# A third tile for raw weights, fixed places for block inputs and g, inputs loaded a block ahead, and stores issued later, in a fused attention and MLP kernel

## The chip, the cores and the metric

The kernel runs on one core of a Trainium2 chip. The metric is the device time in microseconds (us) of one execution; the number compared is the median over runs. TensorE is called PE in the profile, VectorE DVE, ScalarE ACT, GpSimd POOL, and SyncE, from whose queue every load and store of this kernel is issued, SP.

## The reference

Four batches of eight heads go through an attention with 512 local and 32 global tokens (a local token sees the global ones and a window of 32 to either side), then through two MLPs. Here is what the two MLPs compute, with x of 4 x 544 = 2176 tokens by 512:

```
h = np.maximum(x @ w_in, 0.0)          # 512 x 2048
x = h * h @ w_out                      # 2048 x 512
a = x @ w1;  b = x @ w2                # 512 x 1024 each
y = (a * b @ w3) @ w_out2              # 1024 x 1024, 1024 x 512
```

The weights arrive as 64-bit floats.

## The kernel before

**Numbers.** Every product on PE is made of three passes in a fast fp32 mode over a high and a low part of both factors (`PASSES`), so each tensor that PE reads is kept as a pair of parts, written by ACT (the high part, a cast) and DVE (the low part, a subtraction).

**Conversions.** The 72 weight tiles of 128 x 512 come as 64-bit raw tiles (`wraw`, 512 KB each). `conv(n)` turns one into a pair: two ACT instructions read the raw tile (L399 and L402, in `conv_a`), two DVE instructions follow (L407 and L412, `conv_b`; L412 reads the raw tile last), then POOL adds (L477, or L466 for the last 16), ACT casts (L422) and DVE subtracts (L423). `conv_b(n)` also issues the load of raw tile n + 2, since there are two places with the tag `wraw`. One `conv(n)` is `conv_c(n - 1)`, `conv_b(n)`, `conv_a(n + 1)`, so each raw tile is held from its `conv_a` to the `conv_b` of the next call. For n from 16 on, the first ACT and the first DVE instruction of a conversion are held in the order in which the program was written.

**Blocks.** The 2176 tokens are eight blocks of 256 or 288. The first MLP's 2048 hidden columns are done in two halves. The first half runs over blocks 0 to 7, beside the attention up to block 5; its result is stored to `part_d`, and the pair of each input block to `xs_d`. The second half runs over blocks 0 to 7 again with the weights 16 to 31: the pair comes back from `xs_d` (`load_split`, L512), the partial sum from `part_d` (`load_x`, L650), and the sum goes to `x2_d` (L712). The trace names the stored sum `x_d<-st`.

Blocks 6 and 7 of the first half, and all blocks of the second, are written out by `rows`: for f from 0 to 8 a `h_unit` (12 matmuls into one of two PSUM tiles `h`, then on ACT L521 relu, L522 square to the high part of `g`, L528 square again, then on DVE L127 the low part) and an `x_add` for the f before it (12 matmuls into four `acc`). Between f = 4 and f = 7 the four pieces of the next block's input are split or loaded. These inputs and the eight `g` of a block come from 14 places that are given out in turn (tag `hl`). `end_b` then adds `acc` and the partial sum on DVE (L710), stores, and loads the partial sum of the block after next.

**Work beside the blocks.** `merge` spreads the conversions 16 to 29 over the steps of blocks 6 and 7, and 30 to 71 over the second half. With the conversions 41 to 56 go 16 `w_unit` steps (12 matmuls of 512 columns each), which multiply w3 with the last weight in advance; every second one copies its PSUM tile to SBUF on ACT (L702, tile `ws`, which takes a place of the tag `wraw`) and stores it to `w_d` (L703). The conversions 56 to 71 make w1 and w2 in pairs: the first four pairs are stored at once (`both_d`, `sums_d`, L471 and L472).

**After that** come a and b (products by blocks, seven instead of eight, L727), four passes over the units, and y. In the last pass weight pieces are loaded (L905, L919) and split at steps that the table `LATE_V` sets: a row for each quarter of the pass, a number of steps after each of the seven products.

The order on each engine is not that of the code alone: a scheduler places instructions whose operands are ready by its own reckoning.

Of the kernel before, what the change touches and what calls it, by code (L numbers as in the profile page):

```python
# [9 lines left out]
F32 = mybir.dt.float32  # L10
F32R = mybir.dt.float32r
BF16 = mybir.dt.bfloat16
I32 = mybir.dt.int32
# [36 lines left out]
NB = 288  # L50
NBLK = 2 * B
# [3 lines left out]
def block(i):  # L55
    i %= NBLK
    return S * (i // 2) + HALF * (i % 2), HALF if i % 2 == 0 else S - HALF
# [7 lines left out]
RUNS = (0, 16, PAIRED + 16)  # L65
# [14 lines left out]

AHEAD = ((0, 0, 0, 0, 0, 0, 0), (1, 0, 1, 0, 1, 0, 1), (1, 0, 1, 0, 1, 0, 1), (2, 1, 2, 0, 2, 1, 2))
LATE_W = ((2, 1, 1, 0, 2, 1, 1), (1, 1, 1, 1, 1, 1, 1), (1, 1, 1, 0, 1, 0, 0))
LATE_V = ((1, 0, 0, 0, 0, 0, 0), (2, 1, 2, 0, 2, 1, 1), (2, 1, 2, 0, 2, 1, 2), (0, 0, 0, 0, 0, 0, 0))

SHARED = 6

# [6 lines left out]
def attention_mlp(ctx: ExitStack, tc: tile.TileContext, kq0, kq, vw, wts, mask, ident, out_d):  # L93
    nc = tc.nc
# [7 lines left out]
    sb = ctx.enter_context(pool("sb"))  # L102
    cv_cm, rot_cm, at_cm = pool("cv"), pool("rot", "right"), pool("at", "right")
    cv, rot, at = cv_cm.__enter__(), rot_cm.__enter__(), at_cm.__enter__()
# [36 lines left out]
    x_t = {}  # L141
# [241 lines left out]

    raw_t, mid_t, w_t = {}, {}, {}

    def load_w(n):
        t = pools["cv"].tile([128, 512, 2], I32, tag="wraw", name="wraw", bufs=2)
        if n >= PAIRED:
            k, u = divmod(n - PAIRED, 2)
            at = PAIRED + 2 * (LATE + FIRST)[k] + u  # L390
        else:
            at = n
        nc.sync.dma_start(out=t, in_=wts[at].bitcast(I32).rearrange("p (c w) -> p c w", w=2))
        raw_t[n] = t
# [10 lines left out]
    def conv_b(n):  # L405
        raw, (a, b, _) = raw_t.pop(n), mid_t[n]
        first = nc.vector.tensor_scalar(  # L407
            out=a, in0=a, scalar1=3, scalar2=0x7FFFFFF8, op0=ALU.logical_shift_left, op1=ALU.bitwise_and
        )
        if n >= RUNS[1]:  # L410
            tc.keep_in_program_order(first)
        nc.vector.scalar_tensor_tensor(  # L412
            out=b, in0=raw[:, :, 1], scalar=-(1 << 31), in1=a, op0=ALU.bitwise_and, op1=ALU.bitwise_or
        )
        if n + 1 not in RUNS and n + 2 not in RUNS:
            load_w(n + 2)

    def unit(tag, dtype=F32R):
        return pools[tag].tile([128, 2, 512], dtype, tag=tag, name=tag, bufs=16)
# [40 lines left out]
    def conv_c(n):  # L460
        _, b, m = mid_t.pop(n)
        if n >= PAIRED:
            k, u = divmod(n - PAIRED, 2)
            if u == 0:
                both_t[k] = unit("u1", F32)
            nc.gpsimd.tensor_tensor(out=both_t[k][:, u].bitcast(I32), in0=b, in1=m, op=ALU.add)  # L466
            if u == 1:
                x = both_t.pop(k)
                s = add_up(x, "u1", nc.vector)
                if k < 4:  # L470
                    nc.sync.dma_start(out=both_d[k], in_=x)  # L471
                    nc.sync.dma_start(out=sums_d[k], in_=s)  # L472
                else:
                    for f in split_blocks(FIRST[k - 4], k, x, s, "u1"):
                        f()
            return
        nc.gpsimd.tensor_tensor(out=b, in0=b, in1=m, op=ALU.add)  # L477
        t = w_t[n] = unit(UNITS[n])
        split_w(t, slice(0, 512), b.bitcast(F32))
# [16 lines left out]
    def parts(n):  # L496

        return sb.tile([128, 2, NB], F32R, tag="hl", name="hl", bufs=HL_BUFS)[:, :, :n]

    def of_split(i, k):  # L500
        s, n = block(i)
        return xs_d[:, k, :, s : s + n]

    def split_x(i, k, src):
        t = xh[i, k] = parts(src.shape[-1])
        nc.scalar.copy(t[:, 0], src)
        split_lo(nc.vector, t[:, 1], src, t[:, 0])
        nc.sync.dma_start(out=of_split(i, k), in_=t.bitcast(F32))

    def load_split(i, k):  # L510
        t = xh[NBLK + i, k] = parts(block(i)[1])
        nc.sync.dma_start(out=t.bitcast(F32), in_=of_split(i, k))  # L512

    def h_unit(i, f, w):
        n = block(i)[1]
        h = ps.tile([128, 512], F32, tag="h", name="h", bufs=H_BUFS)[:, :n]
        w = w_t[w]
        chain(h, [(w[:, a, 128 * k : 128 * (k + 1)], xh[i, k][:, b]) for k in range(4) for a, b in PASSES])
        r = sb.tile([128, NB], F32, tag="tmp", name="r", bufs=4)[:, :n]
        g = g_t[f] = parts(n)  # L520
        nc.scalar.activation(r, h, AF.Relu)  # L521
        nc.scalar.activation(g[:, 0], r, AF.Square)  # L522
        if i < SHARED:
            nc.vector.scalar_tensor_tensor(
                out=r, in0=h, scalar=0.0, in1=r, op0=ALU.max, op1=ALU.mult
            )
        else:
            nc.scalar.activation(r, r, AF.Square)  # L528
        split_lo(nc.vector, g[:, 1], r, g[:, 0])
# [29 lines left out]
                    start=(f + k == 0), stop=(f + k == 9),  # L559
                )  # L560

    def rows(i, w_in, w_out, split, end):

        n = block(i)[1]
        steps = []
        for f in range(9):
            if f < 8:
                steps.append(lambda f=f: h_unit(i, f, w_in + f))
            if 4 <= f < 8:
                steps.append(lambda f=f: split(f - 4))  # L570
            if f > 0:
                steps.append(lambda f=f: x_add(i, f - 1, w_t[w_out + f - 1], n))
        steps.append(lambda: [end(d) for d in range(4)])
        return steps

    def of(t, i):
        s, n = block(i)
        return t[:, :, s : s + n]
# [67 lines left out]
    def load_x(i):  # L646

        if i < NBLK:
            t = x_t[i] = sb.tile([128, 4, NB], F32, tag="xb", name="xl", bufs=2)[..., : block(i)[1]]
            nc.sync.dma_start(out=t, in_=of(part_d, i))  # L650

    for i in range(0, NBLK, 2):
        main = []
        for j in (i, i + 1):
            if j >= SHARED:
                main += rows(
                    j, 0, 8, lambda d, j=j: split_a(j + 1, d), lambda d, j=j: end_a(j, d, acc[d])
                )
                continue
            if j > 0:  # L660
                main += [lambda f=f, j=j: h_unit(j, f, f) for f in range(8)]
            main += [lambda d=d, j=j: x_unit_a(j, d) for d in range(4)]
        b = i // 2 + 1
        if b < B:
            if b == 1:
                cv_cm.__exit__(None, None, None)
                cv_cm = pool("sp")
                pools["cv"] = cv_cm.__enter__()
                load_kq(H // 2)
                for k in range(H, H + 4):  # L670
                    load_v(k)
            steps = [s for j in range(4 * b - 1, 4 * b + 4) for s in cycle(j, j < 4 * b + 3, j >= 4 * b)]
            fills = [(steps, 0, len(main) - 5)]
        else:
            for cm in (at_cm, rot_cm, cv_cm):
                cm.__exit__(None, None, None)
            pools["u2"] = ctx.enter_context(pool("u2", "right"))
            cv_cm = pool("cv2")
            pools["cv"] = cv_cm.__enter__()
            load_w(16)  # L680
            load_w(17)
            main.insert(18, lambda: load_x(0))
            fills = [([lambda n=n: conv(n) for n in range(16, 30)], 0, len(main))]
        merge(main, *fills)
# [3 lines left out]

    def w_unit(f, half):
        if half == 0:  # L690
            wacc[f] = ps.tile([128, 512], F32, tag="x", name="wacc", bufs=X_BUFS)
        o = wacc[f]
        w3 = w_t[40 + 2 * f + half]
        for q in range(4):
            for k, (a, b) in enumerate(PASSES):
                mm(
                    o, w3[:, a, 128 * q : 128 * (q + 1)], w_t[32 + 4 * half + q][:, b],
                    start=(half + q + k == 0), stop=(half + q + k == 6),
                )
        if half == 1:  # L700
            t = pools["cv"].tile([128, 512], F32, tag="wraw", name="ws", bufs=2)
            nc.scalar.copy(t, o)  # L702
            nc.sync.dma_start(out=w_d[f], in_=t)  # L703

    def split_b(i, d):
        if i < NBLK:
# [2 lines left out]
    def end_b(i, d):  # L709
        nc.vector.tensor_tensor(out=staged(i, d), in0=acc[d], in1=x_t[i][:, d], op=ALU.add)  # L710
        if d == 3:
            nc.sync.dma_start(out=of(x2_d, i), in_=st_t[0])  # L712
            load_x(i + 2)

    def banks():
# [127 lines left out]
    for i in range(NBLK):  # L843
        main += rows(
            NBLK + i, 16, 24,
            (lambda d, i=i: split_b(i + 1, d)) if i < NBLK - 1 else ops_early,
            lambda d, i=i: end_b(i, d),
        )
    late = [lambda n=n: conv(n) for n in range(30, 34)]
    fill = [lambda n=n: conv(n) for n in range(34, PAIRED + 16)]  # L850
# [6 lines left out]
    end = main.pop()  # L857
    main += [lambda n=n: [ops[0].pop(0)() for _ in range(n)] for n in (2, 3, 3, 2, 2)] + [end]
    merge(main, (late, 0, 12), (fill, 12, len(main) - 27))


    cv_cm.__exit__(None, None, None)
# [241 lines left out]
```

## Time and profile before

| | |
|---|---|
| median of 3 runs | 883.19 us (882.39 to 883.42) |
| profiled execution | 886.19 us, of which 884.4 us lie between its first and last instruction |
| PE busy | 846.0 us, 96% |
| ACT, DVE, POOL busy | 494.1, 590.6, 212.9 us |
| mean granted TensorE clock | 0.988 of full speed |
| DMA | 147.51 MB, mean 167 GB/s |

PE is busy nearly always, so what can be won or lost is told by the few stretches where it stands still or runs at a lower clock; the busy times of the other engines matter only where PE waits for them. The blocks 6 and 7 of the first half fill roughly 320 to 372 us, the second half 372 to 620 us, a and b 622 to 795 us, y the rest.

### The profile page before, as it was taken

How to read it: one execution, taken by the hardware profiler on the slowest of the kernel's cores; microseconds unless marked ns; L12 is line 12 of the kernel's file. 1: busy time of each engine (PE TensorE's matmuls, PEld its weight loads, DVE VectorE, ACT ScalarE, POOL GpSimd, SP SyncE). 2: the span in 40 equal slices, each digit the busy share in tenths (PEclk: the TensorE clock that was granted, in tenths of full speed). 3: DMA queues.
4: the chain of work that ended last, by engine and by line, in shares of the span. 5: the costliest groups of instructions: out<-in, count | busy, mean ns of one | idle time of the engine just before them, and what ended most of it. 6: DMA issues, size and time to landing. Idle time of an engine off the chain costs nothing. (4 is left out here: it accounts for less than half of the span.)

```text
span 884.4 us, 17923 instructions
## 1 busy us (share of the span) xinstructions
PE 846.0 (96%) x6664; PEld 797.8 (90%) x6664; DVE 590.6 (67%) x1617; ACT 494.1 (56%) x1317; POOL 212.9 (24%) x254
## 2 busy tenths in 40 slices
PE   5789999999999999899999999999999999999998
PEld 3678898899989999899988899999999999989998
DVE  6998877777385546555534425597895767789771
ACT  6886666676476668667664635587412211245650
POOL 1442000000001012222222202221247744442000
PEclk9889999999999999989999999999999999999999
DMA  6743624332315047456645547866336643848851
GB/s 237 240 150 107 189 63 127 88 105 80 122 48 173 1 147 235 155 177 202 199 150 177 167 140 236 296 210 218 126 113 235 203 162 105 257 157 309 313 202 51
DMA packets 85303, 147.51 MB, mean 167 GB/s; under 512 B 6112, under 2 KB 58464, under 8 KB 85216
## 3 DMA queue, kind: packets, MB, share of 16 engines
q1 hardware_dynamic: 85216, 146.37, 50.2%
q8 instruction: 52, 0.85, 0.4%
q14 instruction: 35, 0.29, 0.1%
HBM read 100.07 MB, written 46.27 MB: 165 GB/s over the span
## 5 line engine op out<-in xcount | busy, mean ns | idle before, releaser
L138 PE MATMUL h<-hl,u 128*128 128x288 f32 (+1 forms) x1536 | 234.2, 297 | 8.2 <-ACT r L521 4.6
L138 PEld LDWEIGHTS h<-hl,u 128*128 128x128 f32 x1536 | 208.9, 193 | 16.9 <-ACT r L521 7.1
L727 PE MATMUL m<-hl,u 128*128 128x272 f32 x1296 | 172.5, 288 | 3.2 <-DVE r L749 1.3
L727 PEld LDWEIGHTS m<-hl,u 128*128 128x128 f32 x1296 | 165.5, 188 | 4.8 <-DVE r L749 2.1
L557 PE MATMUL acc<-hl,u 128*128 128x256 f32 (+1 forms) x960 | 138.1, 289 | 3.1 <-ACT hl L522 1.8
L557 PEld LDWEIGHTS acc<-hl,u 128*128 128x128 f32 x960 | 128.1, 189 | 5.7 <-ACT hl L522 2.4
L477 POOL TENSOR_TENSOR wt<-wt 128x512 int32<-128x512 int32 x56 | 76.2, 1361 | 229.1 <-DVE wt L412 141.9
L127 DVE TENSOR_TENSOR hl<-r,hl 128x288 fp32r<-128x288 f32 (+1 forms) x128 | 65.6, 519 | 67.0 <-ACT r L528 66.6
L138 PE MATMUL x<-hl,u 128*128 128x288 f32 (+1 forms) x576 | 88.8, 296 | 0.0
L399 ACT ACTIVATE wt<-wraw 128x512 f32<-128x512 f32 x72 | 48.3, 672 | 65.3 <-DMA wraw<-in_wts 61.2
L138 PEld LDWEIGHTS x<-hl,u 128*128 128x128 f32 x576 | 76.6, 189 | 4.1 <-issue 2.2
L727 PE MATMUL m<-u,u 128*128 128x272 f32 x528 | 71.1, 287 | 0.7 <-DVE u L757 0.5
L209 ACT ACTIVATE p<-p,st 128x256 f32<-128x256 f32 x128 | 64.3, 507 | 10.0 <-DVE st L205 9.8
L423 DVE TENSOR_TENSOR u<-wt,u 128x512 fp32r<-128x512 f32 x56 | 39.7, 711 | 44.9 <-ACT u L422 44.2
L727 PEld LDWEIGHTS m<-u,u 128*128 128x128 f32 x528 | 67.6, 188 | 1.5 <-DVE u L757 0.7
L521 ACT ACTIVATE r<-h 128x288 f32<-128x288 f32 (+1 forms) x128 | 49.3, 390 | 33.9 <-PE h L138 33.5
L205 DVE CUSTOM_DVE_ANT_0 p<-sc,mask_sb 128x256 f32<-128x256 f32 x128 | 46.9, 417 | 19.2 <-PE sc L132 18.9
L238 POOL CAST qgp<-kq_hl 64x32 fp32r<-64x32 f32 x48 | 16.2, 338 | 178.9 <-PE sg L138 159.0
L744 ACT COPY r<-m 128x272 f32<-128x272 f32 x40 | 15.4, 384 | 76.4 <-PE m L727 76.3
L889 POOL TENSOR_TENSOR rs<-rs 128x272 f32<-128x272 f32 x64 | 56.4, 892 | 2.7
L412 DVE SCALAR_TENSOR_TENSOR wt<-wraw,wt 128x512 int32<-128x512 int32 x72 | 54.5, 756 | 1.4
L522 ACT ACTIVATE hl<-r 128x288 fp32r<-128x288 f32 (+1 forms) x128 | 53.9, 430 | 2.0
(103 smaller groups left out, 1267.3 us busy)
## 6 DMA issues: line engine op xcount, KB each, us to landing
wraw<-in_wts SPq DMA_DIRECT2D x72, 512.0 KB, 3.9
q_d<-rs SPq DMA_DIRECT2D x16, 952.0 KB, 5.1
rl<-q_d SPq DMA_DIRECT2D x12, 1088.0 KB, 7.5
v_f<-in_vw SPq DMA_DIRECT2D x24, 256.0 KB, 3.0
xs_d<-hl SPq DMA_DIRECT2D x16, 288.0 KB, 3.3
hl<-xs_d SPq DMA_DIRECT2D x16, 288.0 KB, 4.0
x2l<-x_d SPq DMA_DIRECT2D x4, 1088.0 KB, 7.3
out<-u SPq DMA_DIRECT2D x16, 272.0 KB, 3.0
```

The source lines that it names most:

```text
L127: eng.tensor_tensor(out=lo, in0=raw, in1=hi.bitcast(F32), op=ALU.subtract)
L138: mm(o, w, x, start=(k == 0), stop=(k == len(terms) - 1))
L205: nc.vector.tensor_tensor_reduce(out=p[:, n, :], in0=sc[:, n, :], in1=mask_sb[:, 2 * part + n, :], scale=-SCALE, scalar=3.0e38, op0=ALU.ad ...
L209: nc.scalar.activation(p[:, n, :], p[:, n, :], AF.Exp, bias=least[:, n : n + 1], scale=-1.0, accum_out=sums[:, n, 0:1],)
L399: first = nc.scalar.activation(t[0].bitcast(F32), raw[:, :, 1].bitcast(F32), AF.Copy, scale=2.0**-112)
L412: nc.vector.scalar_tensor_tensor(out=b, in0=raw[:, :, 1], scalar=-(1 << 31), in1=a, op0=ALU.bitwise_and, op1=ALU.bitwise_or)
L477: nc.gpsimd.tensor_tensor(out=b, in0=b, in1=m, op=ALU.add)
L521: nc.scalar.activation(r, h, AF.Relu)
L522: nc.scalar.activation(g[:, 0], r, AF.Square)
L557: mm(acc[d], w[:, a, 128 * d : 128 * (d + 1)], g_t[f][:, b], start=(f + k == 0), stop=(f + k == 9),)
L727: mm(o, w, x, start=(i in (1, 6, 5, 4) and k == 0), stop=(k == len(terms) - 1), skip_group_check=(i in (2, 7, 3)),)
L889: sub = lambda o, a, c: nc.gpsimd.tensor_tensor(out=o, in0=a, in1=c, op=ALU.subtract)
```

## The change

**A third raw tile.** From n = 16 on, every third raw tile goes to the first 1024 columns of a tile `wx` (one of the two places of tag `xb`, free by then); the load that `conv_b(n)` issues is that of n + 3. The copies `ws` of the products go to two other parts of `wx`, no longer to a place of `wraw`.

**Part buffer.** The partial sums of blocks i and i + 1 lie side by side in the other `xb` place (`extra["x"]`), so that one is loaded while the other is read, as before in two places.

**Fixed places.** From block 6 on (`fix_places`), the 14 `hl` places are given out by number: four for the input of even blocks, four for odd blocks, six in turn for `g`.

**A block ahead.** The next block's input is split or loaded at f = 0 to 3 of the block instead of 4 to 7 (but not at the last block).

**Later stores.** The stores of `x2_d` and `w_d` are issued at the second `h_unit` of the next block, or at the next `w_unit` pair; those of a pair of w1 and w2 when the next pair begins.

**LATE_V.** In the last pass, one step moves from the first product of the third quarter to the last product of the second.

```diff
-LATE_V = ((1, 0, 0, 0, 0, 0, 0), (2, 1, 2, 0, 2, 1, 1), (2, 1, 2, 0, 2, 1, 2), (0, 0, 0, 0, 0, 0, 0))
+LATE_V = ((1, 0, 0, 0, 0, 0, 0), (2, 1, 2, 0, 2, 1, 2), (1, 1, 2, 0, 2, 1, 2), (0, 0, 0, 0, 0, 0, 0))
...
     def load_w(n):
-        t = pools["cv"].tile([128, 512, 2], I32, tag="wraw", name="wraw", bufs=2)
+        if n >= RUNS[1] and n % 3 == 2:
+            t = extra["w"][:, :1024].bitcast(I32).rearrange("p (c w) -> p c w", w=2)
+        else:
+            t = pools["cv"].tile([128, 512, 2], I32, tag="wraw", name="wraw", bufs=2)
...
-        if n + 1 not in RUNS and n + 2 not in RUNS:
-            load_w(n + 2)
+        ahead = n + (2 if n < RUNS[1] else 3)
+        if ahead < RUNS[1] or RUNS[1] <= n and ahead < RUNS[2]:
+            load_w(ahead)
...
                 if k < 4:
-                    nc.sync.dma_start(out=both_d[k], in_=x)
-                    nc.sync.dma_start(out=sums_d[k], in_=s)
+                    both_t["s"] = k, x, s
...
+    def store_now():
+        for o, t in later:
+            nc.sync.dma_start(out=o, in_=t)
+        later.clear()
+
+    def fix_places():
+
+        fixed.extend(xb_t[SHARED, k] for k in range(4))
+        fixed.extend(parts(NB) for _ in range(10))
+
+    def x_parts(i, k, n):
+
+        t = xb_t[i, k] = fixed[4 * (i % 2) + k] if fixed else parts(NB)
+        return t[:, :, :n]
...
-        g = g_t[f] = parts(n)
+        g = g_t[f] = fixed[8 + f % 6][:, :, :n] if fixed else parts(n)
...
-                steps.append(lambda f=f: h_unit(i, f, w_in + f))
-            if 4 <= f < 8:
-                steps.append(lambda f=f: split(f - 4))
+                steps.append(lambda f=f: (h_unit(i, f, w_in + f), store_now() if f == 1 else None))
+            if at <= f < at + 4:
+                steps.append(lambda f=f: split(f - at))
...
-            t = x_t[i] = sb.tile([128, 4, NB], F32, tag="xb", name="xl", bufs=2)[..., : block(i)[1]]
+            if i == 0:
+                extra["x"] = sb.tile([128, 4, 2 * NB], F32, tag="xb", name="xl", bufs=2)
+            at = NB * (i % 2)
+            t = x_t[i] = extra["x"][..., at : at + block(i)[1]]
...
-            t = pools["cv"].tile([128, 512], F32, tag="wraw", name="ws", bufs=2)
+            at = 1024 + 512 * (f % 2)
+            t = extra["w"][:, at : at + 512]
             nc.scalar.copy(t, o)
-            nc.sync.dma_start(out=w_d[f], in_=t)
+            later.append((w_d[f], t))
...
         if d == 3:
-            nc.sync.dma_start(out=of(x2_d, i), in_=st_t[0])
+            later.append((of(x2_d, i), st_t[0]))
             load_x(i + 2)
```

The change moves instructions on SP and ACT. First SP, where the `w_unit` steps run: each row is a transfer in the order of issue (`w_d<-ws` a product's store, `wraw` or `wx<-in_wts` a raw weight tile, `hl<-xs_d` a piece of the next block's input, `x_d<-st` a block's sum, `xl<-part_d` a partial sum). Before:

```order
L703 DMA w_d<-ws 128x512
L512 DMA hl<-xs_d 128x2x288
L393 DMA wraw<-in_wts 128x1024 x2
L712 DMA x_d<-st 512x1x256
L650 DMA xl<-part_d 128x4x256
L703 DMA w_d<-ws 128x512
L393 DMA wraw<-in_wts 128x1024 x3
L703 DMA w_d<-ws 128x512
L393 DMA wraw<-in_wts 128x1024
L512 DMA hl<-xs_d 128x2x256 x2
```

And of the change, the same transfers:

```order
L513 DMA w_d<-wx 128x512
L398 DMA wraw<-in_wts 128x1024
L540 DMA hl<-xs_d 128x2x256
L398 DMA wraw<-in_wts 128x1024
L540 DMA hl<-xs_d 128x2x256 x3
L398 DMA wx<-in_wts 128x1024
L513 DMA w_d<-wx 128x512
L398 DMA wraw<-in_wts 128x1024
L681 DMA xl<-part_d 128x4x256
L513 DMA x_d<-st 512x1x256
```

The raw loads no longer come in twos and threes behind a product's store, the block's store stands behind the load of the partial sum, and the pieces of an input stand together.

Second ACT, where block 7 ends and the second half begins (`wt<-wraw` is a conversion's reading of the raw tile, `u<-wt` its cast, `st<-acc` a copy of block 7's result, `r<-h` the relu that frees a PSUM tile for PE). Before:

```order
L399 ACTIVATE wt<-wraw 128x512
L402 ACTIVATE wt<-wraw 128x512
L422 CAST u_5078<-wt 128x512
L399 ACTIVATE wt<-wraw 128x512
L402 ACTIVATE wt<-wraw 128x512
L632 COPY st<-acc 128x288 x2
L521 ACTIVATE r<-h 128x256 x2
L522 ACTIVATE hl<-r 128x256 x2
L422 CAST u_5124<-wt 128x512
L528 ACTIVATE r<-r 128x256 x2
```

And of the change:

```order
L549 ACTIVATE r<-h 128x256
L556 ACTIVATE r<-r 128x288
L550 ACTIVATE hl<-r 128x256
L556 ACTIVATE r<-r 128x256
L549 ACTIVATE r<-h 128x256
L428 CAST u_5169<-wt 128x512
L404 ACTIVATE wt<-wraw 128x512
L407 ACTIVATE wt<-wraw 128x512
L660 COPY st<-acc 128x288 x2
L550 ACTIVATE hl<-r 128x256
```

Before, two conversions stand ahead of the first two relus of the new block; now those two relus stand ahead of the conversion, which stands between a relu and its square.

## Rows read from the trace of the kernel before

**Rows 1.** Page, busy time, share of the span and instructions of PE.
```profile
PE 846.0 (96%) x6664; PEld 797.8 (90%) x6664; DVE 590.6 (67%) x1617; ACT 494.1 (56%) x1317; POOL 212.9 (24%) x254
```

**Rows 2.** Busy time per stretch (after engines: granted clock, DMA share, GB/s).
```profile
310.00:440.00 130.00, 126.30 (x965) 124.52 (x965) 70.79 (x139) 91.01 (x208) 34.51 (x27) 0.97 0.57 186
440.00:530.00 90.00, 87.60 (x549) 79.67 (x548) 34.54 (x65) 46.80 (x95) 18.62 (x15) 1.00 0.50 161
530.00:610.00 80.00, 76.53 (x593) 74.56 (x592) 56.69 (x114) 53.27 (x121) 19.61 (x15) 1.00 0.74 247
```

**Rows 3.** Waits, 300 to 620 us: us in total, times, longest.
```profile
ACT wt L399 <- DMA wraw<-in_wts: 51.5, 37, 4.5
...
PE h L138 <- ACT r L521: 4.6, 3, 2.6
...
PE acc L557 <- ACT hl L522: 1.8, 2, 1.5
...
PE acc L557 <- DVE hl L127: 1.4, 2, 0.9
PE h L138 <- DMA hl<-xs_d: 1.3, 2, 1.0
```

**Rows 4.** Timeline of ACT, 364 to 384 us.
```profile
372.85 0.66 ACT L399 ACTIVATE wt<-wraw 128x512 f32<-128x512 f32 x1 [1.63 <-DMA wraw<-in_wts]
...
374.54 0.67 ACT L521 ACTIVATE r<-h 128x256 f32<-128x256 f32 x2
```

**Rows 5.** Timeline of PE, 364 to 384 us.
```profile
374.98 5.28 PE L138 MATMUL h<-hl,u 128*128 128x256 f32 x23 [2.65 <-ACT r L521]
```

**Rows 6.** Busy time per stretch, as rows 2.
```profile
375.00:381.00 6.00, 6.00 (x28) 6.00 (x29) 2.30 (x5) 3.76 (x10) 1.28 (x1) 0.50 0.61 199
```

**Rows 7.** Waits of SP's queue, 300 to 620 us.
```profile
SPq L393 <- DVE wt L412: 124.5, 41, 6.1
...
SPq L393 <- DMA w_d<-ws: 18.9, 8, 5.3
```

**Rows 8.** DMA issues: count, KB each, median us to landing.
```profile
wraw<-in_wts SPq DMA_DIRECT2D x72, 512.0 KB, 3.9
```

**Rows 9.** Timeline of ACT, 480 to 488 us.
```profile
482.87 0.66 ACT L399 ACTIVATE wt<-wraw 128x512 f32<-128x512 f32 x1 [3.52 <-DMA wraw<-in_wts]
```

**Rows 10.** Timeline of PE, 480 to 488 us.
```profile
485.89 0.80 PE L557 MATMUL acc<-hl,u 128*128 128x288 f32 x4 [1.48 <-ACT hl L522]
```

**Rows 11.** Busy time per stretch, as rows 2.
```profile
510.00:535.00 25.00, 25.00 (x179) 23.50 (x178) 5.37 (x13) 9.96 (x23) 2.21 (x2) 1.00 0.38 125
540.00:570.00 30.00, 27.03 (x201) 25.94 (x199) 16.93 (x36) 16.56 (x37) 8.40 (x7) 1.00 0.96 328
```

**Rows 12.** Timeline of PE, 776 to 785 us.
```profile
780.78 1.78 PE L727 MATMUL m<-hl,u 128*128 128x272 f32 x12 [1.00 <-ACT r L744]
```

**Rows 13.** Timeline of ACT, 776 to 785 us.
```profile
776.94 1.45 ACT L422 CAST u<-u 128x512 fp32r<-128x512 f32 x3 [1.97 <-DMA u<-sums_d]
```

**Rows 14.** Waits of SP's queue, 622 to 885 us.
```profile
SPq L905 <- PE m L727: 14.2, 2, 8.9
```

**Rows 15.** Groups by line: shapes, count, busy us, mean ns, idle before.
```profile
L522 ACT ACTIVATE hl<-r 128x288 fp32r<-128x288 f32 (+1 forms) x128 | 53.9, 430 | 2.0
L521 ACT ACTIVATE r<-h 128x288 f32<-128x288 f32 (+1 forms) x128 | 49.3, 390 | 33.9 <-PE h L138 33.5
L399 ACT ACTIVATE wt<-wraw 128x512 f32<-128x512 f32 x72 | 48.3, 672 | 65.3 <-DMA wraw<-in_wts 61.2 <-DVE wt L407 2.3 <-DVE p L216 1.2
L402 ACT ACTIVATE wt<-wraw 128x512 int32<-128x512 uint32 x72 | 47.7, 663 | 2.9 <-DMA wraw<-in_wts 2.9
L422 ACT CAST u<-wt 128x512 fp32r<-128x512 f32 x56 | 34.5, 616 | 21.6 <-POOL wt L477 21.6
L528 ACT ACTIVATE r<-r 128x256 f32<-128x256 f32 (+1 forms) x80 | 33.6, 428 | 1.3
```

**Rows 16.** Busy time per stretch, as rows 2.
```profile
310.00:360.00 50.00, 50.00 (x400) 50.00 (x400) 28.55 (x54) 35.37 (x84) 12.34 (x10) 1.00 0.55 180
```

More of the change, by code (lines that the diff above doesn't have):

```diff
@@ L384, in attention_mlp @@
     raw_t, mid_t, w_t = {}, {}, {}
+    extra = {}
     def load_w(n):
-        t = pools["cv"].tile([128, 512, 2], I32, tag="wraw", name="wraw", bufs=2)
+        if n >= RUNS[1] and n % 3 == 2:
+            t = extra["w"][:, :1024].bitcast(I32).rearrange("p (c w) -> p c w", w=2)
+        else:
+            t = pools["cv"].tile([128, 512, 2], I32, tag="wraw", name="wraw", bufs=2)
         if n >= PAIRED:
@@ L465, in conv_c @@
                 both_t[k] = unit("u1", F32)
+                if "s" in both_t:
+                    o, x, s = both_t.pop("s")
+                    nc.sync.dma_start(out=both_d[o], in_=x)
+                    nc.sync.dma_start(out=sums_d[o], in_=s)
             nc.gpsimd.tensor_tensor(out=both_t[k][:, u].bitcast(I32), in0=b, in1=m, op=ALU.add)
@@ L498, in parts @@
         return sb.tile([128, 2, NB], F32R, tag="hl", name="hl", bufs=HL_BUFS)[:, :, :n]
+    fixed, later = [], []
+    def store_now():
[5 more added lines that the diff above has]
+        fixed.extend(parts(NB) for _ in range(10))
+    xb_t = {}
+    def x_parts(i, k, n):
+        t = xb_t[i, k] = fixed[4 * (i % 2) + k] if fixed else parts(NB)
+        return t[:, :, :n]
     def of_split(i, k):
@@ L504, in split_x @@
     def split_x(i, k, src):
-        t = xh[i, k] = parts(src.shape[-1])
+        t = xh[i, k] = x_parts(i, k, src.shape[-1])
         nc.scalar.copy(t[:, 0], src)
@@ L510, in load_split @@
     def load_split(i, k):
-        t = xh[NBLK + i, k] = parts(block(i)[1])
+        t = xh[NBLK + i, k] = x_parts(i, k, block(i)[1])
         nc.sync.dma_start(out=t.bitcast(F32), in_=of_split(i, k))
@@ L560, in x_add, with rows @@
                 )
-    def rows(i, w_in, w_out, split, end):
+    def rows(i, w_in, w_out, split, end, at=0):
         n = block(i)[1]
@@ L655, in attention_mlp @@
             if j >= SHARED:
+                if j == SHARED:
+                    main.append(fix_places)
                 main += rows(
@@ L679, in attention_mlp @@
             pools["cv"] = cv_cm.__enter__()
-            load_w(16)
-            load_w(17)
+            extra["w"] = sb.tile([128, 8 * NB], F32, tag="xb", name="wx", bufs=2)
+            for k in range(16, 19):
+                load_w(k)
             main.insert(18, lambda: load_x(0))
@@ L690, in w_unit @@
         if half == 0:
+            store_now()
             wacc[f] = ps.tile([128, 512], F32, tag="x", name="wacc", bufs=X_BUFS)
@@ L846, in attention_mlp @@
             (lambda d, i=i: split_b(i + 1, d)) if i < NBLK - 1 else ops_early,
-            lambda d, i=i: end_b(i, d),
+            lambda d, i=i: end_b(i, d), 0 if i < NBLK - 1 else 4,
         )
@@ L859, in attention_mlp @@
     merge(main, (late, 0, 12), (fill, 12, len(main) - 27))
+    store_now()
     cv_cm.__exit__(None, None, None)
```

## The prediction

> **What bounds the kernel now.** I read the page first. PE is busy for 96% of the span [rows 1], so the time is PE's work plus the moments in which PE stands still or runs slowly. No edit adds or removes a matmul; only those moments can change. The change lies between 310 and 610 us (blocks 6 and 7, then the second half) and, with one step, in the last pass of a and b. So I next read the busy time by stretch [rows 2]. PE is idle 130.0 - 126.30 = 3.70 us from 310 to 440, 90.0 - 87.60 = 2.40 us to 530, and 80.0 - 76.53 = 3.47 us to 610: 9.57 us in all. The list of waits gives the same, 4.6 + 1.8 + 1.4 + 1.3 = 9.1 us, and says for whom: 7.8 us of it are for results of ACT, or of DVE behind ACT, and 1.3 us for a block input [rows 3].
>
> The next question is what ACT was doing. It waited 51.5 us in 37 waits for raw weight tiles to land [rows 3]. ACT works in order, and a conversion stands between the relus that PE needs. The longest stall shows the whole path: at 372.85 ACT gets its raw tile after a wait, only at 374.54 does it come to the relus [rows 4], and PE, which had both PSUM tiles `h` full, starts again at 374.98 after 2.65 us [rows 5]. Then PE runs at a granted clock of 0.50, the 1.2 GHz level, until 381 [rows 6]: 6 us at half speed lose another 6 x 0.5 = 3.0 us. At 482.87 the same: ACT waits 3.52 us for a raw tile [rows 9], and PE waits 1.48 us for the `g` that ACT makes behind it [rows 10].
>
> Why is the tile late? SP's queue waits 124.5 us in 41 waits for L412, the last reader of a raw tile, before it may load the next one into its place [rows 7]. From issue to landing a load takes 3.9 us [rows 8]. The rate that PE would allow: two blocks are 2 x 192 = 384 matmuls, and 400 went through in 50 us without idle time [rows 16], so two blocks take 48 us, and 14 conversions in them come every 48 / 14 = 3.4 us. A load of 3.9 us that starts one call ahead of its use is late almost every time; this is the loop that the change opens. In the `w_unit` stretch the loads wait a further 18.9 us in 8 waits for the store of a product, since `ws` takes a raw place [rows 7].
>
> **The change part by part.** *Third raw tile.* The load is now issued two calls ahead, 2 x 3.4 = 6.8 us before its use against 3.9 us to landing. From 310 to 440 I take the whole loss as gone: 3.70 idle + 3.0 of half clock = 6.7 us. Bounds: 0 if ACT is late for another reason, 6.7 at most.
>
> *Own place for the products, stores later.* The three raw places no longer wait for `w_d`, and SP no longer stops at a store whose data isn't there: in the order of the change a store stands after work that is long done. From 440 to 530: 2.4 us, bounds 0 and 2.4.
>
> *The pairs, 530 to 610.* The loss is 3.47 us. Here the DMA engines are themselves nearly full, a share of 0.96 at 328 GB/s from 540 to 570, while from 510 to 535 they moved only 125 GB/s [rows 11]: the loads came late and then all together. Steadier loads and stores a pair later should use that slack, but a full DMA can keep some landings late. I take 2.4, about 70%; bounds 0 and 3.47.
>
> *Hidden loss.* The ends of matmuls are modelled, so idle time understates a stall. By count, 80 us at 8 matmuls per us would hold 640; there were 593 from 530 to 610, 47 short or 5.9 us, against 3.47 idle. From 360 to 440 there were 965 - 400 = 565 [rows 2, 16], 75 short or 9.4 us, against the 6.7 above. So up to 2.4 + 2.7 = 5.1 us more could be won, if the mix of widths and missing records explain none of it. I take 1.0.
>
> *Inputs a block ahead, fixed places.* Of the 1.3 us of waits for inputs [rows 3] all is inside the idle time already counted. The four pieces of an input are issued half a block, some 12 us, earlier, into the places of the block before last, whose last reader is done. The split for block 7 moves from f = 4 to 7 to f = 0 to 3: four casts of the size of L522, 4 x 0.43 = 1.7 us of ACT [rows 15], four subtractions and four stores. ACT is busy 35.37 of 50 us there [rows 16], so I cost it at nothing; without that cover it is 1.7 us. Six places for `g` instead of a share of 14: a place is needed again six `h_unit` steps later, and by the order PE runs at most three of them ahead of the `x_add` that reads it. I cost it at nothing.
>
> *New waits.* A load into `wx` waits for L412 as one into `wraw` does; behind it in SP's queue stand pieces of the next input, which have half a block to spare. The load of the partial sum waits for the last `end_b`, and the block's store now stands behind it: that store is read only after the second half. The first load of `x2_d` takes the place of `wx` and waits for conversion 71, and the loads of the sums stand behind it; before, that place was free a block earlier. Conversion 71 is placed before block 7 begins, so I cost this at nothing; uncovered it would delay the start of a by a landing, no less than the 3.9 us of a raw tile [rows 8].
>
> *LATE_V.* In the last pass PE waits 1.00 us for a copy on ACT [rows 12] that stands behind casts which waited 1.97 us for `sums_d` to land [rows 13]. The change issues that load one step, 1.78 us [rows 12], earlier. But the loads ahead of it also wait for PE to release the tile, up to 8.9 us [rows 14], and an earlier issue doesn't help those. Bounds 0 and 1.0, I take 0.5.
>
> **The sum.** 6.7 + 2.4 + 2.4 + 1.0 + 0.5 = 13.0 us. The profiled execution, 886.19 us with a span of 884.4, would become 873.2. It lies 3.0 us above the median of the runs, 883.19, so I forecast a median of 870.2.
>
> **The rivals.** *A: landings stay late.* More loads in flight share the same engines, and each lands later. For it speaks the share of 0.96 [rows 11]; against it the 0.57 and 0.50 of the other two stretches [rows 2]. If the pairs keep all their loss and the middle stretch half: 6.7 + 1.2 + 0.5 = 8.4, a time of 874.8. If in addition one stall of 2.65 us with its 3.0 us at the lower clock stays: 8.4 - 5.65 = 2.75, 880.4. The Trainium skill, in DMA: Bandwidth & Descriptors, section "Issuing engines are not separate DMA queues", says that transfers run on the same 16 engines and interleave, whoever started them; by that rule a third load in flight adds no bandwidth where they are full, and the 2.4 of the pairs would be 0, for 872.6. The trace agrees that they are full there, at 0.96, and shows them with room just ahead, at 0.38 [rows 11].
>
> *B: ACT becomes the bound, and it is slower.* Without the waits for raw tiles, conversions press on ACT. In blocks 6 and 7 the sums of durations are 16 x (0.390 + 0.430 + 0.428) = 20.0 us for the `h_unit` steps and 14 x (0.672 + 0.663 + 0.616) = 27.3 us for conversions [rows 15], 47.3 us of PE's 48. The order of the change even puts a conversion between a relu and its square. If each of 56 conversions delays a `g` so that PE stops 0.5 us, that is 28 us against 13.0, a time of 898. It decides from 13.0 / 56 = 0.23 us per conversion. Against it: from 310 to 360 PE had no idle time with ACT at 71% [rows 16], its instructions overlap at their ends, and in the later stretches it is busy for 46.80 of 90 and 53.27 of 80 us [rows 2].
>
> *C: nothing changes.* If L412 itself is late, because DVE works in order behind PE and ACT, the third place only fills later and ACT waits as long: 883. For it speaks that SP's 124.5 us of waits are all for DVE [rows 7]; against it, that DVE is busy for only 162 of the 300 us [rows 2] and that its own lateness mostly comes from ACT's.
>
> **How the numbers follow.** Forecast (9 to 17 us won) 0.68; A (3 to 9 won) 0.17; C 0.05; B 0.08; more than 17 won 0.02. 0.2% is 1.8 us, about what a measurement of this kernel can tell from no change. Faster is the forecast, A and the last case, 0.87; same is C, 0.05; slower is B, 0.08. The range goes from 866, all the idle time with two thirds of the hidden loss, to 878.5, most of A; the likeliest case alone is 866 to 874.
>
> **What would show it.** Right: ACT's waits for raw tiles fall from 51.5 us to under 15; PE's idle time from 310 to 610 falls from 9.57 to under 3.5; the clock stays at 1.00 there; loads of SP's L398 wait no more for `w_d`. For A: the waits go but for a stretch of DMA share over 0.95. For B: ACT over 90% busy, and PE waits for L550 or L549 with conversions just ahead on ACT. For C: SP still waits 100 us for L417 and ACT's waits stay. The prediction fails if a stall over 2 us appears at a new place and the clock falls behind it, or if PE's work between stalls is slower than 8 matmuls per us.

## The result, and the profile after

The changed kernel takes 871.16 us (median of 4 runs, 868.21 to 871.65), the kernel before 882.79 us (4 runs, 880.58 to 883.42): a ratio of 0.9866, 95% interval 0.9838 to 0.9894. The forecast was 870.2 us, faster, with a range of 866.0 to 878.5. The profiled execution took 871.15 us, 15.0 us less than that of before, and shows where it came from.

The page of the changed kernel, busy time of PE and the granted clock by slices (the row that answers to [rows 1]):

```profile
PE 839.0 (97%) x6664; PEld 793.6 (91%) x6664; DVE 605.1 (70%) x1617; ACT 497.2 (57%) x1317; POOL 216.1 (25%) x254
...
PEclk9999999999999999999999999999999999999999
```

The same number of matmuls; no slice has a lower clock now. The three stretches of [rows 2], and one in which the DMA engines are nearly full, in the changed kernel (after the engines: granted clock, DMA share, GB/s):

```profile
310.00:440.00 130.00, 130.00 (x993) 127.67 (x992) 87.68 (x149) 97.99 (x217) 39.93 (x30) 1.00 0.67 216
440.00:530.00 90.00, 90.00 (x612) 84.36 (x611) 37.55 (x70) 49.13 (x104) 18.15 (x14) 1.00 0.51 165
530.00:610.00 80.00, 79.27 (x616) 78.42 (x615) 60.63 (x125) 56.30 (x133) 17.25 (x12) 1.00 0.65 225
...
520.00:545.00 25.00, 25.00 (x201) 25.00 (x201) 17.38 (x36) 15.71 (x35) 8.18 (x7) 1.00 0.94 325
```

PE's idle time from 310 to 610 us is 0 + 0 + 0.73 us, where it was 9.57 [rows 2]. In the same 300 us, 993 + 612 + 616 = 2221 matmuls begin, where 965 + 549 + 593 = 2107 did [rows 2]: 114 more, at 8 per us 14.3 us, nearly the whole difference of the two executions. (All 192 matmuls of 512 columns lie in these 300 us in both kernels, so the 114 are narrow ones, and their rate may be used.)

The waits of the changed kernel, 300 to 610 us (in total, times, longest), which answer to [rows 3]:

```profile
ACT r L549 <- PE h L138: 47.5, 41, 4.6
...
ACT wt L404 <- DMA wraw<-in_wts: 3.2, 2, 2.7
...
ACT wt L404 <- DMA wx<-in_wts: 0.9, 1, 0.9
...
PE h L138 <- ACT r L549: 0.7, 2, 0.4
```

ACT's waits for raw tiles went from 51.5 us in 37 waits [rows 3] to 3.2 + 0.9 = 4.1 us in 3. ACT now comes to its relus early: it waits 47.5 us for PE's `h`, and PE waits 0.7 us for ACT.

SP's queue in the same stretch, and the loads of raw tiles (count, KB each, median us from issue to landing), in the changed kernel:

```profile
SPq L398 <- DVE wt L417: 115.9, 46, 4.8
...
SPq L513 <- ACT wx L738: 25.2, 8, 9.0
```

```profile
wraw<-in_wts SPq DMA_DIRECT2D x53, 512.0 KB, 4.2
wx<-in_wts SPq DMA_DIRECT2D x19, 512.0 KB, 3.7
```

Two things to see. A load takes no less time than before, 4.2 and 3.7 us against 3.9 [rows 8]: it isn't faster, it is asked for earlier. And SP still waits 115.9 us for L417 (124.5 before, [rows 7]), though nobody feels it any more: with a third place the load that it holds is needed one conversion later, and ACT's wait for raw tiles shows that it is in time. SP's waits for `w_d` before a raw load are gone, as expected; but a product's store still stops SP for 25.2 us until its copy is made.

The stalls that the new `LATE_V` was meant for lie in the last pass. The timelines of PE and of ACT there, in the changed kernel:

```profile
764.37 1.76 PE L763 MATMUL m<-hl,u 128*128 128x272 f32 x12 [0.39 <-ACT r L780]
766.99 1.76 PE L763 MATMUL m<-hl,u 128*128 128x272 f32 x12 [0.86 <-DVE r L785]
```

```profile
760.96 1.45 ACT L428 CAST u<-u 128x512 fp32r<-128x512 f32 x3 [1.78 <-DMA u<-sums_d]
...
762.78 0.93 ACT L428 CAST u<-u 128x512 fp32r<-128x512 f32 x2
```

And of ACT in the kernel before, the casts that answer to the second line:

```profile
779.20 0.93 ACT L422 CAST u<-u 128x512 fp32r<-128x512 f32 x2 [0.49 <-DMA u<-w_d]
```

The wait for the copy on ACT fell from 1.00 us [rows 12] to 0.39, but the casts ahead of it still wait 1.78 us for `sums_d` (1.97 before, [rows 13]). What went is another wait ahead of the copy: before, two casts waited a further 0.49 us for pieces of `w_d`, and now they wait for nothing.

### The profile page after: what moved, and what is told of

Same layout as the page of the kernel before. It is cut to its first block, busy times and chain, and to the rows that moved or that the text cites. A ratio compares the mean times of both kernels' runs of the same rounds, so it can differ in the third digit from the quotient of the medians.

```text
span 869.4 us, 17937 instructions
## 1 busy us (share of the span) xinstructions
PE 839.0 (97%) x6664; PEld 793.6 (91%) x6664; DVE 605.1 (70%) x1617; ACT 497.2 (57%) x1317; POOL 216.1 (25%) x254
## 5 line engine op out<-in xcount | busy, mean ns | idle before, releaser
L127 DVE TENSOR_TENSOR hl<-r,hl 128x288 fp32r<-128x288 f32 (+1 forms) x128 | 75.1, 590 | 57.6 <-ACT r L556 56.6
L926 POOL TENSOR_TENSOR rs<-rs 128x272 f32<-128x272 f32 x64 | 56.6, 895 | 2.7
L286 PE MATMUL tp<-ident_sb,p 128*128 128x128 f32 x256 | 43.0, 296 | 9.2 <-DVE p L216 9.1
L925 POOL TENSOR_TENSOR rs<-rs 128x272 f32<-128x272 f32 x32 | 28.7, 899 | 92.4 <-DVE rs L793 92.4
```

The costliest lines, as they stand in the source:

```text
L127: eng.tensor_tensor(out=lo, in0=raw, in1=hi.bitcast(F32), op=ALU.subtract)
L286: nc.tensor.transpose(tp[:, k, :], p[:, t % 2, 128 * half : 128 * (half + 1)], ident_sb)
L926: sub = lambda o, a, c: nc.gpsimd.tensor_tensor(out=o, in0=a, in1=c, op=ALU.subtract)
```

## The experiments

Theory: the loop of the raw tiles, a load that is asked for too late, held ACT and through it the relus that PE needs; the third tile opens it. Rivals: the products' own place and the later stores did it; or the new order of the instructions (inputs a block ahead, fixed places) did it, and the raw tiles' lateness was harmless. Diffs are against the changed kernel. Ratios are to the kernel before on the same chip, with 95% intervals; "idle" is PE's from 310 to 610 us in the profiled execution.

**The change once more** (changed_again), beside which the next three ran.

> The changed kernel as it is, beside the next three for a common measure. All theories: 871 us, a ratio to the kernel before of 0.985 to 0.988.

0.9867 [0.9844, 0.9889], median 869.71 us against 881.62; idle 0.54 us.

**Two raw tiles, all else of the change** (no_third).

```diff
-        if n >= RUNS[1] and n % 3 == 2:
+        if False:
...
-        ahead = n + (2 if n < RUNS[1] else 3)
+        ahead = n + 2
...
-            for k in range(16, 19):
+            for k in range(16, 18):
```

> The change without the third raw tile: two raw tiles, loads two conversions ahead, the products still in a place of their own. The raw-tile theory (a load of 3.9 us started one call ahead is late, and the third tile is what won the time): most of the 9 us of the first and third stretch come back, 878 to 881 us; ACT waits for raw tiles over 35 us again, and PE's idle time from 310 to 610 us is 5 us or more. The SP theory (what freed the loads is that SP's queue no longer stops at stores and that inputs go ahead): 871 to 874 us, ACT's waits for raw tiles under 20 us. Between 874 and 878: both have a part.

0.9946 [0.9925, 0.9968], 876.95 us: 7.2 us are lost against the change. That is less than the raw-tile theory wanted and falls in the band for both. Its waits, 300 to 610 us, and its busy time by stretch:

```profile
ACT wt L404 <- DMA wraw<-in_wts: 47.2, 38, 3.3
...
PE h L138 <- ACT r L549: 3.9, 5, 1.0
```

```profile
310.00:440.00 130.00, 128.26 (x981) 125.70 (x980) 76.18 (x144) 95.47 (x211) 37.60 (x29) 1.00 0.62 199
440.00:530.00 90.00, 90.00 (x601) 83.72 (x600) 36.06 (x72) 49.59 (x105) 18.14 (x14) 1.00 0.55 179
530.00:610.00 80.00, 77.26 (x597) 75.96 (x597) 58.29 (x123) 57.03 (x135) 18.92 (x13) 1.00 0.66 216
```

ACT's waits for raw tiles are nearly all back, 47.2 us of 51.5, but PE's idle time is 4.48 us, not 9.57: the stall of 2.65 us [rows 5] isn't there. The third tile is the larger part, and not the whole.

**The products' copy in a raw place, stored at once** (ws_raw), third tile kept.

```diff
-            at = 1024 + 512 * (f % 2)
-            t = extra["w"][:, at : at + 512]
+            t = pools["cv"].tile([128, 512], F32, tag="wraw", name="ws", bufs=2)
...
-            later.append((w_d[f], t))
+            nc.sync.dma_start(out=w_d[f], in_=t)
```

> The change with the products' copies again in a place of the raw tiles, stored at once as before; the third raw tile stays. The raw-tile theory with its term of 2.4 us for this edit: 872 to 874 us, with waits of the loads for the products' stores in SP's queue again. If the third raw tile alone covers the stretch of the products: 871 us, no difference. The SP theory: 874 us or more, since SP stops at these stores for some 30 us again.

0.9860 [0.9839, 0.9881], 869.82 us: no loss. Its waits in SP's queue and those of ACT, 300 to 610 us:

```profile
SPq L398 <- DMA w_d<-ws: 11.3, 6, 2.7
```

```profile
ACT wt L404 <- DMA wraw<-in_wts: 14.0, 10, 3.2
```

Raw loads wait for `w_d` again, 11.3 us, and ACT for raw tiles, 14.0 us, and PE is idle 0.22 us: the third tile covers it.

**Inputs at f = 4 to 7 again, places still fixed** (inputs_late).

```diff
-    def rows(i, w_in, w_out, split, end, at=0):
+    def rows(i, w_in, w_out, split, end, at=4):
...
-            lambda d, i=i: end_b(i, d), 0 if i < NBLK - 1 else 4,
+            lambda d, i=i: end_b(i, d), 4,
```

> The change with the next block's input split or loaded at f = 4 to 7 again, places still fixed. The raw-tile theory: this edit was worth at most the 1.3 us of waits for inputs, so 871 to 872.5 us. The SP theory: 874 us or more, with pieces of an input standing between the raw loads again and PE waiting over 2 us for inputs.

0.9881 [0.9858, 0.9904], 871.08 us; 1.4 us over the change measured beside it, less than the intervals can tell; idle 1.36 us, all of it from 530 to 610 us. Its busy time in the first and the third stretch, the one wait of PE that makes up most of the idle time, and ACT where block 7 ends:

```profile
310.00:440.00 130.00, 130.00 (x995) 127.79 (x995) 87.76 (x148) 96.94 (x219) 39.06 (x30) 1.00 0.66 216
...
530.00:610.00 80.00, 78.64 (x614) 78.14 (x613) 58.32 (x127) 56.77 (x134) 19.91 (x13) 1.00 0.70 236
```

```profile
PE h L138 <- ACT r L549: 1.4, 1, 1.4
```

```profile
368.59 0.37 ACT L549 ACTIVATE r<-h 128x256 f32<-128x256 f32 x1
...
371.35 0.67 ACT L404 ACTIVATE wt<-wraw 128x512 f32<-128x512 f32 x1
```

There is no stall at the end of block 7: though the inputs are late, the first relu of the new block stands ahead of the conversion.

**The third tile alone** (third_only), with what was kept beside it: the partial sums side by side, and the copies of the products in `wx` (by ws_raw these bring nothing once there is a third tile). Inputs late, places in turn, stores at once, the old table.

```diff
...
-                    both_t["s"] = k, x, s
+                    nc.sync.dma_start(out=both_d[k], in_=x)
+                    nc.sync.dma_start(out=sums_d[k], in_=s)
...
-    def rows(i, w_in, w_out, split, end, at=0):
+    def rows(i, w_in, w_out, split, end, at=4):
...
-                if j == SHARED:
-                    main.append(fix_places)
...
```

> The change cut down to the third raw tile and what it needs (the tile that holds it and the products' copies, the two partial sums side by side): inputs at f = 4 to 7 from places given out in turn, stores issued at once, the old table. Raw-tile theory: the third tile alone brings nearly all, 870 to 873 us, with ACT's waits for raw tiles under 20 us. The theory that the parts only work together: 875 us or more, since pieces of an input and stores stand between the loads in SP's queue again.

0.9900 [0.9869, 0.9932], 874.15 us against 881.76: 7.6 us, between the two expectations. ACT's waits of L404 for raw tiles are 5.6 us. Part of what it lacks against the change is seen where block 7 ends. Timelines of ACT and of PE of this kernel:

```profile
371.11 0.70 ACT L661 COPY st<-acc 128x288 f32<-128x288 f32 x2 [1.46 <-PE acc L586]
371.79 0.62 ACT L428 CAST u<-wt 128x512 fp32r<-128x512 f32 x1
372.31 0.67 ACT L404 ACTIVATE wt<-wraw 128x512 f32<-128x512 f32 x1
372.88 0.66 ACT L407 ACTIVATE wt<-wraw 128x512 int32<-128x512 uint32 x1
373.45 0.64 ACT L550 ACTIVATE r<-h 128x256 f32<-128x256 f32 x2
```

```profile
373.87 2.41 PE L138 MATMUL h<-hl,u 128*128 128x256 f32 x18 [1.02 <-ACT r L550]
```

The raw tile is there (L404 waits for nothing), but a cast and a conversion stand ahead of the two relus in ACT's order, and PE loses 1.02 us. In the changed kernel's order both relus stand ahead of that cast and conversion.

**All but the third tile** (rest_only): no_third, with the products back in raw places and stored at once.

> The change without the third raw tile and without the products' own place, so with two raw places that the products share as before; inputs a block ahead, fixed places, later stores and the new table stay. The run without the third tile gave 877 us. If the products' own place is worth its 2.4 us where there are but two raw tiles: 878 to 880 us, with loads waiting for the products' stores for over 10 us in SP's queue. If not: 877 us.

0.9949 [0.9922, 0.9976], 878.66 us against 881.76. SP's wait before a raw load, and the busy times:

```profile
SPq L398 <- DMA w_d<-ws: 14.2, 7, 3.7
```

```profile
310.00:440.00 130.00, 126.50 (x965) 123.23 (x963) 73.08 (x137) 91.57 (x204) 36.24 (x28) 1.00 0.62 203
440.00:530.00 90.00, 87.21 (x559) 79.63 (x560) 35.05 (x67) 47.50 (x100) 18.12 (x14) 1.00 0.46 149
530.00:610.00 80.00, 78.25 (x613) 77.34 (x612) 60.87 (x125) 56.69 (x133) 20.85 (x14) 1.00 0.71 244
```

Where block 7 ends, ACT and PE of this kernel:

```profile
369.79 0.38 ACT L549 ACTIVATE r<-h 128x256 f32<-128x256 f32 x1
...
372.26 0.67 ACT L404 ACTIVATE wt<-wraw 128x512 f32<-128x512 f32 x1 [1.65 <-DMA wraw<-in_wts]
```

```profile
372.11 2.05 PE L138 MATMUL h<-hl,u 128*128 128x256 f32 x16
374.15 1.76 PE L585 MATMUL acc<-hl,u 128*128 128x256 f32 x12
```

The raw tile is as late as in [rows 4], 1.65 us, and PE works on without a wait, since a relu of the new block stands ahead of the conversion. But the lateness shows elsewhere: from 310 to 440 us PE is idle 3.50 us in shorter waits, 3.70 before, and 8.04 us from 310 to 610. This execution took 881.05 us, near the upper end of this kernel's runs (876.37 to 881.46), so the gain of 3.1 us rests on the median of the runs, and its trace doesn't show where it comes from.

The parts add up: 7.6 us for the third tile, 3.1 for the rest, 10.7, against 10.6 (881.76 - 871.12) for the next kernel, which has all but the later stores. The partial sums side by side are in both parts; no run takes them out. With two raw tiles the products' place does show: 2.79 us idle from 440 to 530, and none in no_third. In time the two kernels can't be told apart by their ratios.

**Stores at once** (stores_now) and **the old table** (old_late_v), each alone.

```diff
-                    both_t["s"] = k, x, s
+                    nc.sync.dma_start(out=both_d[k], in_=x)
+                    nc.sync.dma_start(out=sums_d[k], in_=s)
...
-            later.append((w_d[f], t))
+            nc.sync.dma_start(out=w_d[f], in_=t)
...
-            later.append((of(x2_d, i), st_t[0]))
+            nc.sync.dma_start(out=of(x2_d, i), in_=st_t[0])
```

> The change with every store issued at once as before. Raw-tile theory: no more than 1 us, 870 to 871.5 us, since with a third tile the loads have time to stand behind a store. SP theory: 873 us or more.

0.9864 [0.9832, 0.9895], 871.12 us: nothing. SP stops for the products' copies 25.1 us, as in the changed kernel.

```diff
-LATE_V = ((1, 0, 0, 0, 0, 0, 0), (2, 1, 2, 0, 2, 1, 2), (1, 1, 2, 0, 2, 1, 2), (0, 0, 0, 0, 0, 0, 0))
+LATE_V = ((1, 0, 0, 0, 0, 0, 0), (2, 1, 2, 0, 2, 1, 1), (2, 1, 2, 0, 2, 1, 2), (0, 0, 0, 0, 0, 0, 0))
```

> The change with the old table for the last pass of a and b. My term was 0.5 us, bounds 0 and 1.0: 870 to 871 us, with the stall of 1.00 us for the copy on ACT back in the third quarter of the last pass. If the table does nothing: the stalls there are those of the change, within 0.2 us in all.

0.9864 [0.9830, 0.9897], 870.92 us: nothing. Timeline of PE in the last pass with the old table:

```profile
764.63 1.76 PE L763 MATMUL m<-hl,u 128*128 128x272 f32 x12 [0.43 <-ACT r L780]
767.26 1.76 PE L763 MATMUL m<-hl,u 128*128 128x272 f32 x12 [0.86 <-DVE r L785]
```

The same two stalls, 0.43 and 0.86 us, as with the new table (0.39 and 0.86). The stall of 1.00 us [rows 12] shrank for another reason: with the old table, too, the two casts ahead of the copy no longer wait for `w_d`. Which edit brings those pieces in time no run here isolates.

**Places in turn, inputs late** (places_in_turn): third tile, later stores and new table kept.

```diff
-    def rows(i, w_in, w_out, split, end, at=0):
+    def rows(i, w_in, w_out, split, end, at=4):
...
-                if j == SHARED:
-                    main.append(fix_places)
...
```

> The change with the inputs at f = 4 to 7 and the 14 places given out in turn as before; third raw tile, later stores and the new table stay. The run with the third tile alone was at 0.990 of the kernel before, the one with late inputs in fixed places at 0.988. If the places given out in turn are what the third tile alone still lacks: 0.990 or 873 us, with a stall of about 1 us at the end of block 7. If it is the stores: 0.988 or 871 us, and no such stall.

0.9882 [0.9867, 0.9896], 874.03 us; idle 3.53 us, with the stall at the end of block 7 again. PE there, and the busy time:

```profile
372.53 2.99 PE L138 MATMUL h<-hl,u 128*128 128x256 f32 x23 [1.01 <-ACT r L549]
```

```profile
310.00:440.00 130.00, 128.14 (x975) 124.88 (x974) 87.55 (x147) 94.66 (x214) 37.46 (x30) 1.00 0.62 201
```

This kernel differs from inputs_late in the fixed places alone, and that one has no stall there: it is the fixed places, not the early inputs, that put a relu ahead of the conversion. The next kernel, measured beside this one, took 870.3: some 3.7 us less. Inputs ahead and fixed places together are worth about 3 us (874.15 - 871.12 = 3.0 by the earlier pair). Of the 3.7 us, inputs_late leaves 1.4 to the inputs and so 2.3 to the places, near the 3.53 - 1.36 = 2.2 us of idle time between the two; but both shares are close to what the intervals can tell, and the ratios of the two kernels, 0.9882 and 0.9881, don't show it.

**One step more ahead in the last pass** (late_v_more).

```diff
-LATE_V = ((1, 0, 0, 0, 0, 0, 0), (2, 1, 2, 0, 2, 1, 2), (1, 1, 2, 0, 2, 1, 2), (0, 0, 0, 0, 0, 0, 0))
+LATE_V = ((1, 0, 0, 0, 0, 0, 0), (2, 2, 2, 0, 2, 1, 2), (0, 1, 2, 0, 2, 1, 2), (0, 0, 0, 0, 0, 0, 0))
```

> The change with one more step of the last pass moved ahead: the second loads one product earlier again. If the landing of sums is what still stalls PE there (0.4 and 0.9 us in the change): those stalls fall by half a microsecond or more, the time to 869 to 870.5 us, within what the measurement can tell from none. If the release of the tiles by PE holds the loads, or DVE's own work stalls PE there: the stalls stay and the time is that of the change.

0.9849 [0.9823, 0.9876], 870.3 us against 884.0: no measurable gain over the change. Its timeline of ACT there:

```profile
760.33 1.45 ACT L428 CAST u<-u 128x512 fp32r<-128x512 f32 x3 [1.63 <-DMA u<-sums_d]
```

The pieces still land late, by 1.63 us instead of 1.78 (1.94 with the old table): moving a step in the table hardly moves their arrival.

**The kernel before, two further executions** (before_2 and before_3), for the price of the lower clock.

> The kernel before as it is, for a second trace of it. My term of 3.0 us takes the lower clock behind the stall of 2.65 us as a part of every execution. If so: the stall near 372 us and a granted clock of about 0.5 for some 6 us behind it are seen again. If it belongs to some executions only: the stall is there again, the clock stays at 1.00 from 310 to 440 us, and the term was worth less than 3.0 us in the median.

> As the run before it, a third trace of the kernel before: stall near 372 us in every trace; the lower clock behind it in every trace (term 3.0 us in full), in one of them (part of it), or in none but the first.

880.89 and 876.93 us; idle 8.39 and 5.95 us. The three stretches in the first, and the last of them in the second:

```profile
310.00:440.00 130.00, 126.79 (x984) 124.54 (x983) 72.56 (x141) 92.44 (x209) 36.08 (x28) 1.00 0.58 190
440.00:530.00 90.00, 88.38 (x565) 80.89 (x564) 34.30 (x65) 47.28 (x98) 17.94 (x15) 1.00 0.49 156
530.00:610.00 80.00, 76.44 (x585) 74.16 (x584) 59.08 (x117) 53.55 (x125) 18.80 (x15) 1.00 0.78 259
```

```profile
530.00:610.00 80.00, 78.80 (x610) 77.25 (x609) 60.89 (x121) 55.98 (x131) 18.59 (x14) 1.00 0.78 265
```

The stall at the end of block 7 in the first, then the 6 us of [rows 6] in the first and in the second:

```profile
373.56 2.99 PE L138 MATMUL h<-hl,u 128*128 128x256 f32 x23 [2.44 <-ACT r L521]
```

```profile
375.00:381.00 6.00, 6.00 (x53) 6.00 (x52) 5.13 (x11) 5.19 (x14) 1.29 (x1) 1.00 0.64 205
```

```profile
375.00:381.00 6.00, 6.00 (x53) 6.00 (x53) 5.13 (x11) 4.91 (x14) 1.29 (x1) 1.00 0.61 198
```

The stall is there, 2.44 us (2.38 in the second), but the granted clock stays at 1.00, and 53 matmuls begin where 28 did [rows 6]. The 3.0 us of half clock belong to one of three profiled executions.

## Why the prediction was right, point by point

**The loop of the raw tiles: right, and shown.** Without the third tile 7.2 us are lost; with only the products' own place and the side-by-side partial sums beside it, it wins 7.6. ACT's waits follow it: 4.1 us with it, 47.2 without. In the predicted sum it carried the 6.7 us from 310 to 440 us, and all of the 3.70 idle and the 3.0 of half clock did go, in the pair of traces of the forecast. Not by the third tile alone, though: in third_only PE is still idle 1.87 us there, in no_third 1.74.

**Half clock, 3.0 us: mis-sized for the median.** I took it from one execution and also took the 3.0 us by which that execution lay above the median as something apart, so the same 3.0 may have been subtracted twice. Two further traces have the stall without the lower clock. How often the timed runs have it can't be read from them.

**Products' own place, 2.4 us: the idle time went, the reason was another.** 2.40 us of idle time from 440 to 530 went. But ws_raw, without the place of its own, has none there either; the place helps only while there are two raw tiles (2.79 us idle against 0). The two edits do the same work, and the sum gave each its own stretch. Later stores are worth nothing, and the claim that SP would no longer stop at a store was wrong: 25.2 us of such stops are left, harmless.

**Pairs, 2.4 of 3.47 us: 2.74 went.** That is by the trace of the forecast; before_3 had only 1.20 us to lose there. Rival A is refuted: landings did not get shorter, yet ACT and PE hardly wait for them. From 520 to 545 us the share is 0.94 at 325 GB/s, no more than before at its fullest [rows 11], but PE has no idle time in it. The Trainium skill says, in DMA: Bandwidth & Descriptors, section "Issuing engines are not separate DMA queues", that transfers run on the same 16 engines and interleave, whoever started them. The rows agree with what I drew from that, that a third load adds no bandwidth where the engines are full. My explanation for the rest is that loads asked for earlier use time in which the engines have room: from 310 to 440 they move 216 GB/s, where it was 186 [rows 2]. No run isolates that.

**Hidden loss, 1.0 us: too small.** The count of matmuls says 14.3 us for the region; idle time and half clock that went are 8.84 + 3.0 = 11.8. So 2.4 us more were won than idle time shows. The bound of 5.1 was too wide: 14 of the matmuls counted from 360 to 440 had 512 columns and took 0.25 us each, so 1.7 us of the 9.4 were the mix of widths, and 3.4 is left, which holds. The missing 1.4 here and the 0.3 of the pairs stand against the doubtful 3.0 of the clock and the 0.5 of the table: that errors of either sign leave the forecast of 870.2 within 1 us of 871.16 is partly luck.

**LATE_V, 0.5 us: nothing.** The bound of 0 held: the pieces hardly land earlier when their step moves, some 0.15 us for each step. Whether PE's release of the tiles holds them, as I argued, no run shows.

**Inputs ahead and fixed places, at nothing: about 3 us.** Here the working failed. I priced only the waits for inputs and the work that moves. What counted was ACT's order at the end of block 7: rest_only and no_third, with raw tiles still late, have no stall there, and third_only, with raw tiles in time, has one of 1.02 us. The stall of 2.65 us had two causes in a row, a late raw tile and a conversion standing ahead of the relus; I put all of it to the first. The order comes with the fixed places: with late inputs the stall is 0 in fixed places (inputs_late) and 1.01 us in places given out in turn. With late tiles, removing that one stall did not remove the loss: in rest_only PE is idle nearly as long in other places. The waits that I feared at the start of a did not come: the changed kernel's PE has no wait from 590 to 636 us.

**Rival B refuted:** ACT is busy 97.99 of 130 us, 75%, and PE has no idle time there. The 47.3 of 48 us of its working are summed durations, but instructions overlap at their ends: in the rows of third_only a conversion's two instructions last 0.67 and 0.66 us and begin 0.57 us apart.

**Rival C refuted, by the time; its sign was badly chosen.** SP does still wait 115.9 us for L417, which I had named as a mark of C. A wait's length says nothing of whether it ends before the need; the sign that decides is the consumer's wait, ACT's 4.1 us.

No version here beats the change by more than the intervals: ws_raw, stores_now, old_late_v and late_v_more all lie with it.

## What to carry to other kernels

Compare the time from a load's issue to its landing with the distance between its issue and its use, and count places by that; a load needn't get faster to stop hurting. When a wait of PE ends on another engine, look both at what that engine waited for and at what stood ahead in its order: here the third tile cut the stall of 2.65 us to 1.02, and the order alone removed it at that place but left waits elsewhere. To tell two edits apart, compare runs that differ in one of them. Don't price a lower clock from a single execution, and check idle time against a count of matmuls.

## What the runs showed of the hardware

- After a stall of PE of 2.65 us the granted clock was 0.50 (the 1.2 GHz level) for 6 us in one execution; after 2.44 us at the same place in another it stayed at 1.00 (2.4 GHz), and after 2.38 us in a third. In inputs_late it stayed there behind 1.4 us. Whether the two tenths of a microsecond or something else decided isn't known.
- Idle time understates the loss: in the stretch of 300 us, 8.8 us of idle time less and 3.0 us of half clock less went with 14.3 us' worth of matmuls more. Against before_2 it is 8.39 - 0.73 = 7.7 us of idle time and 2221 - 2134 (984 + 565 + 585) = 87 matmuls, 10.9 us.
- A load of 512 KB took 4.2 and 3.7 us to land (`wraw`, `wx`) in the kernel with three places to load into, and 3.9 in that with two, in the median over the whole execution; among the loads from 300 to 610 us, 4.0 and 3.6 against 3.7. At DMA shares of 0.51 to 0.67 the third place hardly slowed the loads.
